# A transformer block on one core: the first transposed blocks copied in two pieces, two first projections done block by block, and a new list of tasks

## The chip, the cores and the metric

The kernel runs on one core of one Trainium2 chip. The metric is the device time of one execution in microseconds. Each of the core's engines (TensorE or PE, VectorE or DVE, ScalarE or ACT, GpSimd or POOL, and SyncE or SP, which here only issues DMAs) runs its own instructions in order, and they meet at semaphores.

## The reference, cut to what matters

```python
x = A_x                                     # 1 x 2048 x 640, bf16
h  = x + A(layernorm(x))
h2 = h + silu(layernorm(h) @ w1) @ w2       # 640 -> 1728 -> 640

def A(x):                                   # 32 heads of 20, 4 segments of 512 tokens
    q, k, v = x @ wq, x @ wk, x @ wv
    for s in range(4):                      # M (20x20 a head) and z carry over
        p = softmax(qs @ ks.T * scale + causal_mask)
        a_mem = (phi(qs) @ M) / (phi(qs) @ z + 1e-6)     # phi(t) = t+1 if t>0 else exp(t)
        o = g * a_mem + (1 - g) * (p @ vs)               # g = sigmoid(beta), a head
        M, z = M + phi(ks).T @ vs, z + sum(phi(ks))
    return o @ wo
```

## The kernel before, in words

**Staging.** The 2048 tokens are 16 blocks of 128, four to a segment; a block lies in the 128 partitions. The weights stay in on-chip memory, and every array goes to and from DRAM once. A block is normalized in `layer_norm` (statistics `st` and `r`, then `ap`, which writes bf16 rows `xn_rot`), and its transpose (feature on the partitions) is what the projections and the first FFN product read. The first four blocks are transposed on TensorE: `tp` multiplies by the identity, five matmuls of 128 columns into two PSUM banks, and `te` copies the five chunks into `hT` (lines 786 and 787: one instruction on ScalarE or on VectorE). All other blocks are transposed by a DMA, `tr` (line 792). `wq` and `wk` are rearranged after loading, one chunk of 128 rows at a time (`re_w`, lines 691 and 693), so that four heads stand at partitions 0, 32, 64 and 96 of a product.

**Attention.** For each segment s, `pr` (line 859) are ten projections of q and k (five chunks c, w = 0 for q and 1 for k), 512 columns each; in segment 0 each is two halves, x (blocks 0 and 1) and y (2 and 3). `qe` (lines 867, 868) copies a product from PSUM. `v` and `ve` do the same for the values. Twelve small DMAs a segment, `vt` (line 899), move the heads that did not fit in the five chunks to three further ones, and `vp` does so for phi(q). For eight groups of four heads: `qk` (line 949) writes scores into four PSUM banks, four heads at a time on four row tiles of TensorE; `e` (line 961) is the exponential on ScalarE, either one instruction over four banks (128x2048, with a + in its name) or two over two banks each (128x1024); `mk` masks the diagonal on GpSimd; `av` multiplies by the values, four column tiles at once; `oe` scales and copies that product, `tn` transposes it back, `nm` normalizes, `ad` adds the memory part. `pha`, `phb` and `ex` make phi; `kt` transposes phi(k) by a DMA (line 1192), `kg` and `kh` gather its left-over heads, and `mz`, `ma`, `mb` update M and z.

**Behind it.** `ot` (line 1249) transposes the attention rows of a block by a DMA, `wo` (line 1257) multiplies them by `wo` into two banks, `rs` adds x. After the second layer norm, `h1` (line 1292, 14 chunks; segment 0 in two halves) and `th`, `s` (silu), then `h2` (line 1334; four tasks a block, `h2_b_0` to `h2_b_3`; the last also reads `w_w2_5` if the block is odd), `o` (residual) and `out` (store). `w_w1_*` and `w_w2_*` are the loads of the FFN weights (line 580).

**What sets the order.** Every step is a task of a graph. The order of all tasks, the engine of those that have a choice, and the buffers are a list, `ORDER`, of words `name/engine:slots`: A is ScalarE, D VectorE, G GpSimd, S SP; slots are buffer or PSUM bank numbers, in the order in which the task first needs them. `wo11:6` is the product of block 11 in banks 6 and 7. Each engine takes its tasks in the list's order; `Tracker` puts in the semaphore waits that reads, writes and reused buffers need. A PSUM bank can thus be written again only when the engine that read it last is done. `fill29:0` is 29 matmuls on TensorE into bank 0 that nobody reads, at the start. DMAs are issued by SP or ScalarE, in their place in that engine's list.

The tasks that the prediction follows: `w_w2_5` and `h2_1_3`, `ot2` and `wo2`, the twelve `vt` of segment 1 and `qk13a0` (the first scores that read them), `n1_tr8` to `n1_tr11` and `pr220`, `av24`, `av25`, `oe24`, `oe25` and `wo11`, and at the front `n1_tp0`, `n1_tp1`, their copies `te` and the first projections.

Of the kernel before, what the change touches and what calls it, by code (L numbers as in the profile page):

```python
# [324 lines left out]
D = 640  # L325
# [6 lines left out]
NC = D // 128  # L332
# [10 lines left out]
SPLIT0 = tuple((c, w) for c in range(5) for w in range(2))  # L343
HALVES = True
# [117 lines left out]
def build(nc, es, A_x, A_wq, A_wk, A_wv, A_wo, A_beta, B_x, B_w1, B_w2, out):  # L462
# [340 lines left out]
    def declare_front(s):  # L803
# [5 lines left out]
        for i in range(4):  # L809
            layer_norm("n1_", 4 * s + i, X[4 * s + i], [0], xTa, xT_, i, k0 + P["ln1"] + P["ln1s"] * i if s else -30 + i)  # L810
# [599 lines left out]
```

## Time and profile before

| | |
|---|---|
| time, median of 3 runs (lowest, highest) | 300.31 us (299.82, 300.44) |
| the profiled execution's own time | 301.21 us |
| its span, and what lies around it | 299.5 us, 1.7 |
| granted TensorE clock | 1.00 |
| busy in the span: PE, DVE, ACT, POOL | 286.4, 219.3, 219.2, 137.9 us |
| exponentials on ACT (line 961) | 152.2 us |

The page's line "span" gives the stretch from the first to the last recorded instruction, and engines' busy time as a share of it. In a timeline a row is a run of like instructions: start and length in us, engine, line, what it computes, how many; in brackets stands how long the engine was idle just before it and what ended that. SPq is the queue of DMA issues on SP. The lines themselves stand in the prediction.

### The profile page before, as it was taken

Reading aid. Unit: us, or ns where it says so; the run is one execution under the profiler, and the core shown is the slowest. Engines: PE = TensorE matmul, PEld = TensorE weight load, DVE = VectorE, ACT = ScalarE, POOL = GpSimd, SP = SyncE. Lnnn points to the kernel's source line nnn. Section 1 sums busy time; section 2 is a strip of 40 time slices with the busy share of each in tenths; the row PEclk is TensorE's granted clock in tenths of the full one; section 3 lists DMA queues with packets and bytes.
Section 4 is the critical chain, followed back from the end, with each engine's and each line's share of the span. In section 5 each row is a group of like instructions: output and inputs, shape, how many; then the busy total and the mean of one; then the engine's idle time right before and its main releaser. Section 6 shows DMA issues by size and latency. Waiting matters only on the chain.

```text
span 299.5 us, 7397 instructions
## 1 busy us (share of the span) xinstructions
PE 286.4 (96%) x2980; PEld 167.7 (56%) x2980; DVE 219.3 (73%) x499; ACT 219.2 (73%) x266; POOL 137.9 (46%) x256
## 2 busy tenths in 40 slices
PE   8898799999998999999999999999999999999997
PEld 6685454545664554666653444456665457754575
DVE  4798768877777878899689875757977677835522
ACT  4985998999997989999889888978786840013500
POOL 4247873545643688636465445625675620200000
DMA  7945745264835241052552300173242012321002
GB/s 214 363 137 100 176 87 182 47 166 124 149 62 85 45 109 30 4 104 50 98 145 55 75 2 2 20 91 70 51 71 46 9 37 53 90 66 44 25 22 88
DMA packets 49905, 25.38 MB, mean 85 GB/s; under 512 B 39488, under 2 KB 48032, under 8 KB 49872
## 3 DMA queue, kind: packets, MB, share of 16 engines
q1 hardware_dynamic: 47944, 22.74, 33.9%
q10 hardware_dynamic: 1928, 2.18, 2.6%
q8 instruction: 23, 0.38, 0.6%
q14 instruction: 10, 0.08, 0.1%
HBM read 10.41 MB, written 2.62 MB: 44 GB/s over the span
## 4 chain that ended last, share of the span: by engine, by line
PE 67%; DVE 9%; SPq 7%; ACT 7%; DMA 5%; issue 2%; POOL 0%; ACTq 0%; DVEq 0%
PE ps_all L1334 18%; PE ps_all L1292 14%; PE ps_all L859 9%; PE ps_all L1257 7%; PE ps_all L949 6%; ACT PT L961 5%; PE ps_all L993 5%; PE ps_all L820 4%; SPq L899 4%; DMA x_tok<-in_A_x_dram 2%; DMA oT<-otok 2%; PE ps_all L1023 1%; SPq L792 1%; DVE stt L741 1%; SPq L580 1%
## 5 line engine op out<-in xcount | busy, mean ns | idle before, releaser
L961 ACT ACTIVATE PT<-ps_all 128x1024 bf16<-128x1024 f32 (+1 forms) x114 | 152.2, 1369 | 15.5 <-PE ps_all L949 14.8
L972 POOL TENSOR_SCALAR_AFFINE_SELECT PT<-PT 128x512 bf16<-128x512 bf16 x128 | 81.3, 646 | 66.6 <-ACT PT L961 64.6
L1334 PE MATMUL ps_all<-w_sb,sT 128*128 128x320 bf16 (+2 forms) x462 | 65.3, 295 | 0.6 <-DMA w_sb<-in_B_w_dram 0.4
L1292 PE MATMUL ps_all<-hT,w_sb 128*128 128x512 bf16 (+1 forms) x325 | 62.5, 337 | 0.5 <-DVE sT L1307 0.3
L1301 ACT ACTIVATE th<-ps_all 128x512 f32<-128x512 f32 (+2 forms) x70 | 33.3, 502 | 38.9 <-PE ps_all L1292 33.1
L1334 PEld LDWEIGHTS ps_all<-w_sb,sT 128*128 128x128 bf16 x462 | 43.1, 98 | 19.2 <-issue 1.3
L1307 DVE SCALAR_TENSOR_TENSOR sT<-th,ps_all 128x512 bf16<-128x512 f32 (+2 forms) x70 | 38.0, 561 | 17.1 <-ACT th L1301 16.0
L1292 PEld LDWEIGHTS ps_all<-hT,w_sb 128*128 128x128 bf16 x325 | 29.8, 98 | 26.1 <-issue 3.3
L762 POOL TENSOR_TENSOR rst<-rst,eps_c 128x1 f32<-128x1 f32 x32 | 18.6, 580 | 27.7 <-DVE rst L756 26.2
L741 DVE BATCH_NORM_STATS2 stt<-x_tok 128x6 f32<-128x320 bf16 x62 | 27.2, 480 | 1.7 <-DMA x_tok<-in_A_x_dram 1.3
L1257 PE MATMUL ps_all<-wo_sb,oT 128*128 128x320 bf16 x160 | 24.3, 299 | 1.2 <-DMA oT<-otok 0.6
L1055 POOL TENSOR_TENSOR otok<-on 128x320 bf16<-128x320 bf16 x24 | 19.1, 799 | 11.1 <-DVE on L1047 11.1
L1347 DVE SCALAR_TENSOR_TENSOR x_tok<-ps_all,x_tok 128x640 bf16<-128x640 f32 (+3 forms) x18 | 13.1, 744 | 13.8 <-PE ps_all L1334 13.8
L1047 DVE TENSOR_TENSOR on<-ps_all,rd 128x640 bf16<-128x640 f32 x24 | 19.8, 824 | 0.9
L1257 PEld LDWEIGHTS ps_all<-wo_sb,oT 128*128 128x128 bf16 x160 | 14.9, 98 | 8.7 <-issue 2.1
L820 PE MATMUL ps_all<-wv_sb,xT 128*128 128x320 bf16 x120 | 18.3, 299 | 0.9 <-ACT PT L961 0.5
L859 PE MATMUL ps_all<-xT,wkr 128*128 128x512 bf16 x75 | 18.6, 380 | 0.1
L868 DVE CAST QK<-ps_all 128x512 bf16<-128x512 f32 x22 | 15.0, 688 | 4.8 <-PE ps_all L859 4.6
L768 DVE TENSOR_SCALAR xn_rot<-x_tok,mvt,rst 128x640 bf16<-128x640 bf16 x32 | 15.5, 489 | 3.8 <-POOL rst L762 2.6
L859 PE MATMUL ps_all<-xT,wqr 128*128 128x512 bf16 x75 | 18.2, 380 | 0.0
L1265 DVE TENSOR_TENSOR x_tok<-ps_all,x_tok 128x640 bf16<-128x640 f32 x16 | 13.1, 817 | 7.0 <-PE ps_all L1257 6.9
L993 PE MATMUL ps_all<-PT,Vx 128*32 128x512 bf16 (+3 forms) x384 | 16.4, 301 | 0.0
(104 smaller groups left out, 336.6 us busy)
## 6 DMA issues: line engine op xcount, KB each, us to landing
w_sb<-in_B_w_dram SPq DMA_DIRECT2D x5, 432.0 KB, 4.4
w_sb<-in_B_w_dram SPq DMA_DIRECT2D x3, 480.0 KB, 4.0
x_tok<-in_A_x_dram SPq DMA_DIRECT2D x2, 640.0 KB, 6.9
out_dram<-x_tok SPq DMA_DIRECT2D x8, 160.0 KB, 1.9
out_dram<-x_tok ACTq DMA_DIRECT2D x7, 160.0 KB, 1.8
wo_sb<-in_A_wo_dram SPq DMA_DIRECT2D x1, 800.0 KB, 10.8
QKV<-QK SPq DMA_DIRECT2D x11, 72.0 KB
sT<-in_A_wq_dram SPq DMA_DIRECT2D x2, 320.0 KB, 3.9
```

The lines of the kernel that those rows point to most:

```text
L741: T.add(DV, lambda e, hh=hh: e.bn_stats(out=stt[:, s, 6 * hh:6 * hh + 6], in_=xb[:, 320 * hh:320 * hh + 320]), reads=R((xa, xsub)), writes ...
L820: fns.append(lambda e, c=c, hh=hh: e.matmul(bank(ps, hh)[:, 0:320], lhsT=xT_[:, c, 128 * i:128 * i + 128], rhs=wv_sb[:, c, 320 * hh:320 * ...
L859: fns = [lambda e, kc=kc: e.matmul(bank(ps)[:, lo:hi], lhsT=wt[:, kc, c, :], rhs=xT_[:, kc, lo:hi], start=(kc == 0), stop=(kc == NC - 1)) ...
L961: T.add(AC, lambda e: e.activation(out=pt[:, pta.slot, q0:q0 + nq, 0:width], in_=sc3[:, b0:b0 + nq, 0:width], func=ACT.Exp, scale=SCALE), ...
L972: T.add(PO, lambda e: e.affine_select(out=v, in_=v, pattern=[[0, 4], [1, 128]], compare_op=ALU.is_ge, fill=0.0, base=0, channel_multiplier ...
L993: fns.append(lambda e, j=j, r=r, h=h, pa=pa, pt=pt, co=co, q0=q0, ji=ji: e.matmul(bank(po)[32 * r:32 * r + 32, q0:hi], lhsT=Vx[:, vx.slot, ...
L1047: T.add(DV, lambda e: e.tensor_tensor(out=on[:, ona.slot, :, :].rearrange("p b (x e) -> p b x e", e=DH), in0=v[:, :, :, 0:DH], in1=r2.unsq ...
L1257: fns.append(lambda e, c=c, hh=hh: e.matmul(bank(ps, hh)[:, 0:320], lhsT=oT[:, c, 128 * i:128 * i + 128], rhs=wo_sb[:, c, 320 * hh:320 * h ...
L1292: fns = [lambda e, c=c: e.matmul(bank(ps)[:, lo:hi], lhsT=w1_sb[:, c, 128 * f:128 * f + 128], rhs=hT[:, c, lo:hi], start=(c == 0), stop=(c ...
L1301: T.add(AC, lambda e: e.activation(out=th[:, tha.slot, lo:hi], in_=bank(ps)[:, lo:hi], func=ACT.Tanh, scale=0.5), reads=R((ps, [0])), writ ...
L1307: T.add(DV, lambda e: e.scalar_tensor_tensor(out=sT[:, f, lo:hi], in0=th[:, tha.slot, lo:hi], scalar=1.0, in1=bank(ps)[:, lo:hi], op0=ALU. ...
L1334: fns.append(lambda e, f=f, t0=t0, fr=fr, hh=hh, n=n: e.matmul(bank(pa, hh)[:, 0:n], lhsT=sT[:, f, t0:t0 + 128], rhs=w2_sb[:, fr, c0 + 320 ...
```

## The change

Three things change.

First, the copies of the transposed blocks 0 and 1 are each two tasks: `te0a` takes chunks 0 to 2, `te0b` chunks 3 and 4. The list puts te0a, te0b and te1a on ScalarE and te1b on VectorE; before, te0 was on VectorE and te1 on ScalarE. What reads `hT` in segment 0 now waits for both pieces (`XS`).

Second, the two projections named in `FIRST`, pr010x and pr040x (the query halves of chunks 1 and 4), are done block by block: five matmuls of 128 columns for block 0 and five for block 1, where there were five of 256 columns. The first five wait for block 0 alone.

Third, the whole list is another one. It begins with `fill30:7`, 30 filler matmuls where there were 29, and ends with `fill2:2` for `fill2:6`. 40 of the 80 exponentials of score tiles are one instruction over four banks, where 46 were.

```diff
+FIRST = ("010x", "040x")
...
-            def e_te(eng):
...
-                T.add(eng, f, reads=R((ps, [0])), writes=R((dstA, [i])))
-            G.task(f"{tag}te{b}", {AC: act_c(640), DV: dve_c(640)}, e_te, [(ps, [0])], [(dstA, [i])], prio)
+            for k, (c0, c1) in enumerate(((0, 3), (3, 5)) if b < 2 else ((0, 5),)):
+                ww = [(i, 0), (i, 1)] if b >= 2 else [(i, k)]
+
+                def e_te(eng, c0=c0, c1=c1, ww=ww):
...
+                    T.add(eng, f, reads=R((ps, [0])), writes=R((dstA, ww)))
+                n = 128 * (c1 - c0)
+                G.task(f"{tag}te{b}" + ("ab"[k] if b < 2 else ""), {AC: act_c(n), DV: dve_c(n)}, e_te, [(ps, [0])],
+                       [(dstA, ww)], prio)
...
+        XS = lambda bs: list(bs) if s else [(i, h) for i in bs for h in (0, 1)]
...
+                        if tag in FIRST:
+                            for i in range(b0, b1):
+                                t0 = 128 * i
+                                T.run(PE, [lambda e, kc=kc, t0=t0: e.matmul(
+                                    bank(ps)[:, t0:t0 + 128], lhsT=wt[:, kc, c, :], rhs=xT_[:, kc, t0:t0 + 128],
+                                    start=(kc == 0), stop=(kc == NC - 1)) for kc in range(NC)],
+                                    R((xTa, XS([i])), (W[wk_], [c])), R((ps, [0])))
+                            return
-                        T.run(PE, fns, R((xTa, range(b0, b1)), (W[wk_], [c])), R((ps, [0])))
+                        T.run(PE, fns, R((xTa, XS(range(b0, b1))), (W[wk_], [c])), R((ps, [0])))
```

Of the list, two lines near the tasks av24, av25 and wo11:

```diff
-ot8 mk26b_0 av24:6 oe24/A:0 vt39/S kh23/D phb330 phb221 kt22:0 e26a2 qk26e0:0 e26e2:0 wo11:6 e26e0 mk26e_0 mk26e_256
+h2_4_2 mk25b_0 mk25b_384 qk26a0:2 e26a2:4 h2_4_3 o4 vt34/S kg22/G av25:7 e26a0 mk26a_0 av24:5 vt31/S oe25/A:1 oe24/D:0
```

In the old list av25:7 and oe25/D stand in the line before the first of these.

**SP's queue around ot3 and ot2.** The next two pieces are SP's rows from ot3 (before: the row ahead of the first one shown) to ot2, the last row in each. L899 and L914 are the `vt`, L792 and L798 the DMA transposes `n1_tr`, L1192 and L1207 is kt13, L1249 and L1264 is `ot`, L580 and L581 are loads of w2. Before:

```order
L792 DMA_TRANSPOSE xT<-xn_rot 128x5x128
L899 DMA QKV<-QK 12x3x1024
L899 DMA QKV<-QK 8x2x1024 x2
L792 DMA_TRANSPOSE xT<-xn_rot 128x5x128
L899 DMA QKV<-QK 8x1x1024 x3
L792 DMA_TRANSPOSE xT<-xn_rot 128x5x128
L1192 DMA_TRANSPOSE phiKt<-phiK 128x4x128
L899 DMA QKV<-QK 8x2x1024
L899 DMA QKV<-QK 12x3x1024
L580 DMA w_sb<-in_B_w_dram 64x640
L899 DMA QKV<-QK 8x1x1024
L1249 DMA_TRANSPOSE oT<-otok 128x5x128
```

Of the changed kernel, again from the row after ot3:

```order
L914 DMA QKV<-QK 12x3x1024
L581 DMA w_sb<-in_B_w_dram 128x3x640
L914 DMA QKV<-QK 8x1x1024
L798 DMA_TRANSPOSE xT<-xn_rot 128x5x128 x2
L914 DMA QKV<-QK 8x1x1024
L914 DMA QKV<-QK 8x2x1024
L798 DMA_TRANSPOSE xT<-xn_rot 128x5x128
L1207 DMA_TRANSPOSE phiKt<-phiK 128x4x128
L914 DMA QKV<-QK 8x2x1024 x2
L914 DMA QKV<-QK 12x3x1024
L914 DMA QKV<-QK 8x1x1024
L1264 DMA_TRANSPOSE oT<-otok 128x5x128
```

The load `L580 DMA w_sb<-in_B_w_dram 64x640`, which is w_w2_5, is no longer among them: it now stands twenty rows ahead of ot2 (row 31 of SP, ot2 being row 51 in both). One three-chunk load of w2 (w_w2_3) stands there now. Of the transposes n1_tr, three stand here in both lists; the fourth (n1_tr9 before, n1_tr10 now) follows behind ot2, before it ahead of kt12 and now behind it.

**ScalarE's first rows.** L786 and L790 are the `te`, L691 and L692 the rearrangement of wq and wk, L867 and L882 the copies `qe` of projections. Before:

```order
L733 ACTIVATE otok,mvt<-x_tok 128x640
L736 ACTIVATE otok,mvt<-x_tok,mvt 128x640
L786 ACTIVATE hT<-ps_all 128x5x128
L691 ACTIVATE wqr<-sT 128x5x4x20
L691 ACTIVATE wqr<-sT 128x5x4x12
L691 ACTIVATE wqr<-sT 128x5x4x20
L691 ACTIVATE wqr<-sT 128x5x4x8
L691 ACTIVATE wqr<-sT 128x5x4x4
L867 ACTIVATE w_sb<-ps_all 128x256
L691 ACTIVATE wkr<-sT 128x5x4x20
L691 ACTIVATE wkr<-sT 128x5x4x12
L867 ACTIVATE w_sb<-ps_all 128x256 x6
```

Of the changed kernel:

```order
L734 ACTIVATE otok,mvt<-x_tok 128x640
L737 ACTIVATE otok,mvt<-x_tok,mvt 128x640
L790 ACTIVATE hT<-ps_all 128x3x128
L790 ACTIVATE hT<-ps_all 128x2x128
L790 ACTIVATE hT<-ps_all 128x3x128
L692 ACTIVATE wqr<-sT 128x5x4x20
L692 ACTIVATE wqr<-sT 128x5x4x8
L692 ACTIVATE wqr<-sT 128x5x4x4
L882 ACTIVATE w_sb<-ps_all 128x256 x2
L692 ACTIVATE wkr<-sT 128x5x4x20
L692 ACTIVATE wkr<-sT 128x5x4x12
L882 ACTIVATE w_sb<-ps_all 128x256 x5
```

One copy of five chunks became three pieces, and two of the rearranged rows of wq went to VectorE.

**ScalarE's exponentials in segment 0.** L961 and L976 are the exponentials of scores, 128x2048 if over four banks and 128x1024 if over two; L834 is `ve`, L1222 and L1237 `ma00`, L874 and L889 `ex`. Before, from e0y1 on:

```order
L961 ACTIVATE PT<-ps_all 128x2048
L647 ACTIVATE zf<-beta_bc 128x32
L834 ACTIVATE Vx<-ps_all 128x32x20
L961 ACTIVATE PT<-ps_all 128x1024 x2
L961 ACTIVATE PT<-ps_all 128x2048
L961 ACTIVATE PT<-ps_all 128x1024 x2
L961 ACTIVATE PT<-ps_all 128x2048
L1222 ACTIVATE Mz<-ps_all 128x2x84
L961 ACTIVATE PT<-ps_all 128x1024 x2
```

Of the changed kernel, from e0y1 on:

```order
L976 ACTIVATE PT<-ps_all 128x1024 x2
L976 ACTIVATE PT<-ps_all 128x2048 x2
L889 ACTIVATE ex<-w_sb 128x512
L976 ACTIVATE PT<-ps_all 128x1024 x2
L976 ACTIVATE PT<-ps_all 128x2048
L1237 ACTIVATE Mz<-ps_all 128x2x84
L976 ACTIVATE PT<-ps_all 128x1024 x4
L976 ACTIVATE PT<-ps_all 128x2048
```

The exponential of e4x1, two halves before, is one instruction of four banks, and stands directly ahead of that of e4x2; e0y1 is two halves now.

218 lines of the change are left out of this document (109 added, 109 removed).

## The prediction

> **What bounds the kernel now.** I read the page's first line and the busy time of each engine by stage first, to see which engine is short of time where.
>
> ```profile
> span 299.5 us, 7397 instructions
> ...
> 30.00:74.00 44.00, 39.90 (x540) 22.10 (x530) 34.48 (x86) 41.12 (x43) 25.79 (x50) 1.00 0.51 131
> 74.00:86.00 12.00, 11.65 (x155) 7.36 (x153) 8.91 (x22) 11.97 (x17) 7.01 (x16) 1.00 0.65 119
> 86.00:97.00 11.00, 9.91 (x104) 5.40 (x101) 7.97 (x19) 9.13 (x12) 3.71 (x8) 1.00 0.48 79
> 97.00:155.00 58.00, 57.49 (x659) 33.30 (x659) 49.82 (x117) 51.96 (x61) 36.03 (x59) 1.00 0.32 62
> ...
> 240.00:283.00 43.00, 42.88 (x282) 25.14 (x281) 27.08 (x50) 10.48 (x19) 4.24 (x8) 1.00 0.22 51
> ```
>
> The columns are start and end, length, then busy time of TensorE, its weight loads, VectorE, ScalarE and GpSimd, the granted clock (1.00 everywhere), DMA share and GB/s. Three regimes show. From 30 to 86 us ScalarE is the fuller engine: 41.12 of 44 and then 11.97 of 12 us. From 97 us on TensorE is full: 57.49 of 58, and 42.88 of 43 near the end. Between them, at 86 to 97, neither is: TensorE stands still for 1.09 us and ScalarE for 1.87. A reordering can win nothing in the last regime, because TensorE's work is the same; it can win in the gap, and in the first 86 us if it lightens ScalarE.
>
> So next I looked at what TensorE waits for in the gap, in its timeline, and at what the SP queue did before that.
>
> ```profile
> 86.24 0.40 PE L949 MATMUL ps_all<-QK 20*128 20x512 bf16 x4
> 86.57 1.53 PE L1257 MATMUL ps_all<-wo_sb,oT 128*128 128x320 bf16 x10
> ...
> 90.90 1.26 PE L1334 MATMUL ps_all<-w_sb,sT 128*128 128x320 bf16 x8 [0.43 <-DMA w_sb<-in_B_w_dram]
> ...
> 93.13 1.53 PE L1257 MATMUL ps_all<-wo_sb,oT 128*128 128x320 bf16 x10 [0.65 <-DMA oT<-otok]
> ...
> 97.35 0.40 PE L949 MATMUL ps_all<-QKV 20*128 20x512 bf16 x4
> ```
>
> ```profile
> 72.56 0.58 SPq L580 DMA_DIRECT2D w_sb<-in_B_w_dram  x1
> ...
> 74.06 1.23 SPq L1249 DMA_TRANSPOSE oT<-otok  x1
> 75.40 1.22 SPq L792 DMA_TRANSPOSE xT<-xn_rot  x1
> 76.67 2.31 SPq L899 DMA_DIRECT2D QKV<-QK  x3
> 79.02 2.24 SPq L792 DMA_TRANSPOSE xT<-xn_rot  x1
> 81.31 2.00 SPq L899 DMA_DIRECT2D QKV<-QK  x3
> 83.35 1.20 SPq L792 DMA_TRANSPOSE xT<-xn_rot  x1
> 84.60 1.27 SPq L1192 DMA_TRANSPOSE phiKt<-phiK  x1
> 85.91 1.57 SPq L899 DMA_DIRECT2D QKV<-QK  x2
> 87.52 1.62 SPq L580 DMA_DIRECT2D w_sb<-in_B_w_dram  x1
> 89.19 0.68 SPq L899 DMA_DIRECT2D QKV<-QK  x1
> 89.91 1.21 SPq L1249 DMA_TRANSPOSE oT<-otok  x1
> 91.16 1.28 SPq L792 DMA_TRANSPOSE xT<-xn_rot  x1
> ```
>
> SP issues without a pause: the rows of its timeline join end to end from 74.06 to 91.16. Both things that TensorE waits for are in that queue's tail: w_w2_5 (87.52) feeds h2_1_3 at 90.90, and ot2 (89.91) feeds wo2 at 93.13. So here the length of SP's list is the bound. The two waits sum to 0.43 + 0.65 = 1.08 us.
>
> **The change part by part.** The sum is made against the profiled execution, 301.21 us (its span of 299.5 and 1.7 around it); it lies 0.9 above the median of 300.31, so I take the difference over to the median.
>
> *SP's list from ot3 to ot2.* Before, 14 issues stand from ot3 up to ot2, w_w2_5 among them. Now w_w2_5 is issued some twenty issues earlier, ahead of kt03, and from ot3 up to ot2 stand ot3, eight vt, w_w2_3, three transposes n1_tr and kt13. By the pitches of the rows: ot3 1.34 (74.06 to 75.40), a vt 0.75 ((2.35 + 2.04 + 1.61) / 8), an n1_tr 1.25, kt13 1.31, a w2 load 0.63 (72.56 to the next start, by its row 0.58 and the 0.05 that follows each). That is 1.34 + 6.00 + 3.75 + 0.63 + 1.31 = 13.03 us, so ot2 issues at 74.06 + 13.03 = 87.1, not 89.91: one vt fewer (0.75), and the two slow issues of before, 79.02 (2.24, about 1.0 over its kind) and 87.52 (1.62, 1.0 over), not counted. It landed 3.18 after its issue (next fence), so now at 90.3; wo2, with both waits gone, is wanted at 93.13 - 1.08 = 92.05. The wait goes, and so does that of h2_1_3. If two issues are slow again, ot2 lands at 92.3, and 0.25 stays. I take -1.08, with -0.83 and 0 as the poor ends.
>
> ```profile
> 25.15 3.39 DMA w_sb<-w_sb
> ...
> 89.91 3.18 DMA oT<-otok
> ```
>
> What is late next: qk13a0 at 97.35 needs all twelve vt. The last now follows ot2, kt12, n1_tr10 and vt15: 87.1 + 1.25 + 1.31 + 1.25 + 0.75 = 91.7, landing 3.39 later (a like transfer, the first row) at 95.0, wanted at 96.3. Then n1_tr10 itself, wanted by pr220: issued at 89.7 against 91.16 for the last n1_tr of before. Past 97 TensorE is full, so a shift at 93 reaches the end.
>
> *ScalarE's load before 86 us.* Off it go ve01, ve10, qe120 and ma01, on it comes qe101.
>
> ```profile
> L834 ACT ACTIVATE Vx<-ps_all 128x640 bf16<-128x640 f32 x3 | 2.2, 722 | 0.0
> L867 ACT ACTIVATE QK<-ps_all 128x512 bf16<-128x512 f32 x8 | 4.8, 601 | 0.5 <-PE ps_all L859 0.4
> L1222 ACT ACTIVATE Mz<-ps_all 128x168 f32<-128x168 f32 x2 | 0.6, 308 | 0.1
> ```
>
> 2 x 0.72 + 0.60 + 0.31 - 0.60 = 1.75 us less. VectorE takes it in 34.48 of 44 us. How much arrives is between nothing (another engine holds the stage) and 1.75. Only the stretch of 74 to 86 has no ScalarE idle time at all, and of the moved ones ma01 stands next to it; I take -0.3.
>
> *wo11 near 201.* Before, wo11 writes banks 6 and 7, and the later of the two copies that free them (oe24) is on ScalarE.
>
> ```profile
> 201.29 2.88 PE L1257 MATMUL ps_all<-wo_sb,oT 128*128 128x320 bf16 x20 [0.51 <-ACT oTs L1006]
> ```
>
> Now av24 lies in bank 5, so that wo11 waits for oe25 alone, which comes first. 0 to -0.5; oe25 sits behind an exponential on ScalarE, so -0.2.
>
> *More changes between tile shapes on TensorE.* Counting qk (four row tiles), av and h1_*_13 (four column tiles) and the rest (whole array) in both lists, the shape changes 195 times where it did 192. The four qk matmuls at 86.24 let the next task begin 0.33 later (86.57), though 512 columns at that next row's rate (ten of 320 columns in 1.53 us, 0.48 ns a column) take 0.24: about 0.1 for a change. Three more: +0.3, or 0 where TensorE waits anyway.
>
> *The front.* Block 0's copy, one CAST on VectorE, becomes two on ScalarE; block 1's, one on ScalarE, becomes one on each.
>
> ```profile
> 5.42 0.19 POOL L752 TENSOR_SCALAR rst<-mvt 128x1 f32<-128x1 f32 x1 [0.42 <-ACT otok L736]
> ...
> 6.42 0.37 PEld L777 LDWEIGHTS ps_all<-ident,xn_rot 128*128 128x128 bf16 x5
> ...
> 7.00 0.82 DVE L787 CAST hT<-ps_all 128x640 bf16<-128x640 f32 x1
> ...
> 7.45 0.70 ACT L786 ACTIVATE hT<-ps_all 128x640 bf16<-128x640 f32 x1 [2.12 <-PE ps_all L777]
> ...
> 8.30 2.34 PE L859 MATMUL ps_all<-hT,wqr 128*128 128x256 bf16 x20 [0.89 <-ACT hT L786]
> ...
> 10.15 0.74 DVE L693 COPY wkr<-sT 128x400 bf16<-128x400 bf16 x4 [1.27 <-DMA sT<-in_A_wk_dram]
> ...
> 10.62 1.81 PE L859 MATMUL ps_all<-hT,wkr 128*128 128x256 bf16 x15
> ...
> 10.97 0.89 DVE L741 BATCH_NORM_STATS2 stt<-x_tok 128x6 f32<-128x320 bf16 x2
> ```
>
> ScalarE's three copies are bounded by 0.70 each, and by 0.70 for two together; take 1.2 in all: from about 7.1 to 8.3, against 8.15 before. Block 0 is whole by about 7.9, so pr010x can start on it at about 8.2, when its weights' copies (VectorE, after te1b) are there: a gain of 0.1 at most. One filler more, 30 for 29 (the list has no six fewer), puts the transposes at 6.6; behind that hides that ap0 now stands behind r1 on VectorE, which waits for ScalarE's statistics until 5.42. But whatever is won here meets the key weights, which VectorE gets at 10.15 from the DMA, and blocks 2 and 3, whose statistics start at 10.97: the three projections of k start at 10.62 in either case. I take 0; up to 0.4 late passes there too.
>
> *Queue moves that I cost at nothing.* x8 and w_w1_0 go ahead of the vt on SP, and w_w2_0 ahead of n2_tr1 and n2_tr0, so that a load is issued before the transposes on which the first h1 tasks wait. By the two rows of such loads (72.56 and 87.52) each holds SP for 0.6 to 1.6 us; these are the bounds on the h1 side, beside 0. I take 0, because the h1 tasks fall into the stage of 30 to 74 us, in which ScalarE and not TensorE is the fuller engine and 3.9 of 44 us of TensorE are idle already.
>
> Sum: -1.08 - 0.3 - 0.2 + 0.3 + 0 = -1.28, 301.21 to 299.93, and the median to 299.0.
>
> **The rivals.**
>
> *SP's order does not matter.* The DMA engines are busy for 0.65 of 74 to 86 us; were landing, not issuing, the limit, ot2 would come when it did, and only -0.3 - 0.2 + 0.3 is left: 300.1. Against it: ot2 took 3.18 us to land, of 19 us in the queue. The Trainium skill, "DMA: Bandwidth & Descriptors", section "Issuing engines are not separate DMA queues", says that time on the issuing sequencer is usually small beside the transfer; by that rule this rival is the forecast. The trace differs: 15.85 us of issues stand against 3.18 of landing. Chance 0.10.
>
> *The wait forms anew at qk13a0.* If two issues are slow again, the last vt lands at 97.0, 0.75 late, and 0.25 of ot2's wait stays: -0.28, 300.0. Chance 0.14.
>
> *Slower: the exponentials take turns with TensorE.* A score task whose banks the exponential just before it on ScalarE still reads cannot start until that one ends; ScalarE then idles.
>
> ```profile
> 33.29 3.71 ACT L961 ACTIVATE PT<-ps_all 128x1024 bf16<-128x1024 f32 x3 [0.51 <-PE ps_all L949]
> ...
> 47.48 1.88 ACT L961 ACTIVATE PT<-ps_all 128x2048 bf16<-128x2048 f32 x1 [0.50 <-PE ps_all L949]
> ```
>
> These are two such pairs, e4x3 after e4x2 and e4ya after e3ya. In the new list ten pairs have nothing between them on ScalarE, six before (the first new one: e4x2 after e4x1, one instruction of four banks where it was two halves). Four more at 0.5 are +2.0; with -1.08 + 0.3 that is +1.2, 301.5 for the median. It decides from the third new pair that TensorE has no other work for. Against it: before 86 us the count is two in both. Chance 0.17.
>
> *ScalarE's relief arrives whole:* -1.08 - 1.75 = -2.8, 297.5. Chance 0.08.
>
> **How the numbers follow.** The forecast has 0.51, with its own range of 298.3 to 299.8 (relief 0 to -0.8, shape changes 0 to 0.3). The range of 297.8 to 301.2 holds it, both no-change rivals and the near part of the slow and of the fast one. A measurement of this kernel can tell about 0.2%, 0.6 us. Faster: 0.51 + 0.08, less 0.01 of the forecast's upper end, 0.58. Slower: 0.17 and 0.01 of unnamed ends, 0.18. The same: 0.24.
>
> **What would show it.** Right: ot2 issued 2 us or more sooner after ot3 than 15.85, no DMA named ahead of h2_1_3 and wo2, the k projections still starting near 10.6, wo11's wait under 0.3. Wrong: TensorE waits of half a microsecond on ScalarE's exponentials at new places, a wait of qk13a0 on QKV, hT late at the first h1, or the first k projection past 11.0.

## The result and the profile after

The changed kernel takes 298.33 us (median of 5, 297.27 to 298.85) against 300.31 (299.82 to 300.59) for the kernel before: a ratio of 0.9932, 95% interval 0.9914 to 0.9949. Beside the last three experiments both were timed again: 297.69 (6 runs) against 300.26 (17 runs), 0.9917 (0.9898 to 0.9936). The prediction was 299.0. In the profiled executions the difference is larger, a span of 296.6 against 299.5. In some executions the granted clock falls for a few microseconds and the time is mostly 1 to 2.5 us longer: so in the profiled ones of a_nosplit and a_tr7 (0.87 and 0.86 from 24 to 33 us) and of a_actback (0.58 from 46 to 50 us), of which only stretches outside the fall are compared, and in four of the six of a_actback, whose two at a clock of 1.00 took 301.66 and 302.52.

The stages of the changed kernel, in the columns of the table by stage that the prediction shows:

```profile
span 296.6 us, 7437 instructions
...
30.00:74.00 44.00, 40.44 (x550) 22.80 (x543) 36.63 (x91) 41.45 (x48) 25.50 (x46) 1.00 0.54 117
74.00:86.00 12.00, 11.90 (x160) 7.43 (x158) 11.07 (x26) 11.62 (x17) 7.43 (x13) 1.00 0.76 139
86.00:97.00 11.00, 10.51 (x115) 6.13 (x113) 10.30 (x23) 10.18 (x9) 6.21 (x15) 1.00 0.41 78
97.00:155.00 58.00, 57.61 (x652) 32.86 (x650) 48.44 (x110) 51.40 (x64) 33.72 (x57) 1.00 0.35 74
...
240.00:283.00 43.00, 43.00 (x285) 26.13 (x284) 25.73 (x48) 11.45 (x20) 3.51 (x7) 1.00 0.23 54
```

As the clock is the same and TensorE's work nearly so, the stages that gained are those in which TensorE is busy for longer: 40.44 for 39.90 from 30 to 74 us, 11.90 for 11.65, and 10.51 for 9.91 in the gap. From 97 to 155 and from 240 to 283 us, where TensorE was already full, little was won (57.61 for 57.49, 43.00 for 42.88).

A sharper reading is the start of one and the same task in two traces. The difference of the starts is how far TensorE is ahead; where it changes, time was won or lost. The last three columns are two traces that were taken later: b_unmerge, an experiment whose list is that of before but for six exponentials, and a second profile of the changed kernel.

| task | before | after | lead | b_unmerge | after again | lead |
|---|---|---|---|---|---|---|
| pr011x, first projection of k | 10.62 | 10.50 | -0.12 | 10.66 | 10.64 | -0.02 |
| qk4ya0 | 47.03 | 47.06 | +0.03 | 47.39 | 46.70 | -0.69 |
| qk11a0 | 86.24 | 85.01 | -1.23 | 86.43 | 84.66 | -1.77 |
| wo2 | 93.13 | 90.59 | -2.54 | 92.15 | 90.24 | -1.91 |
| qk13a0 | 97.35 | 94.96 | -2.39 | 96.67 | 94.60 | -2.07 |
| av19 | 151.11 | 148.67 | -2.44 | 150.20 | 148.23 | -1.97 |
| qk25a0 | 183.06 | 181.16 | -1.90 | 182.14 | 180.45 | -1.69 |
| wo11 | 201.29 | 199.02 | -2.27 | 200.37 | 198.30 | -2.07 |
| qk31a0 | 235.20 | 232.77 | -2.43 | 234.28 | 232.06 | -2.22 |
| last h2 | 296.77 | 293.89 | -2.88 | 295.51 | 293.18 | -2.33 |

In both pairs 1.1 to 1.3 us are won between qk4ya0 and qk11a0. In the gap, from qk11a0 to qk13a0, the first pair shows 1.16 and the second 0.30; that is the row on which the prediction's main term stood, and the pairs do not agree on it (further traces of this stage stand under b_w2early). Some 0.3 to 0.5 is lost between av19 and qk25a0, and about 0.4 comes back up to wo11. Behind wo11 the lead grows by another 0.61 and 0.26; no wait of TensorE over 0.15 us stands there in any of the four traces, and where it comes from was not looked into.

The gap in TensorE's timeline of the changed kernel, and SP's queue there (ot3 at 72.98, ot2 at 86.93):

```profile
88.27 2.07 PE L1349 MATMUL ps_all<-w_sb,sT 128*128 128x320 bf16 x14
90.27 0.39 PE L964 MATMUL ps_all<-QK 20*128 20x512 bf16 x4
90.59 1.53 PE L1272 MATMUL ps_all<-wo_sb,oT 128*128 128x320 bf16 x10
...
93.49 0.46 PE L1225 MATMUL ps_all<-Vx,phiKt 128*128 128x84 bf16 x8 [0.37 <-DVE x_tok L1280]
...
94.96 0.39 PE L964 MATMUL ps_all<-QKV 20*128 20x512 bf16 x4
```

```profile
72.98 1.28 SPq L1264 DMA_TRANSPOSE oT<-otok  x1
...
76.56 3.27 SPq L798 DMA_TRANSPOSE xT<-xn_rot  x2
...
83.90 2.99 SPq L914 DMA_DIRECT2D QKV<-QK  x4
86.93 1.21 SPq L1264 DMA_TRANSPOSE oT<-otok  x1
```

Both waits of before are gone, at h2_1_3 and at wo2, and none formed at qk13a0; a new one of 0.37 stands at 93.49, where mz10 writes a bank that VectorE frees late. SP needs 13.95 us from ot3 to ot2, where it needed 15.85; in the second profile it needs 13.33. (The prediction had 13.03; two transposes took 3.27, where it counts 2.50.)

### The profile page after: what moved, and what is told of

Its sections match the earlier page's. It is cut to its first block, busy times and chain, and to the rows that moved or that the text cites. A ratio compares the mean times of both kernels' runs of the same rounds, so it can differ in the third digit from the quotient of the medians.

```text
span 296.6 us, 7437 instructions
## 1 busy us (share of the span) xinstructions
PE 285.0 (96%) x2991; PEld 167.6 (56%) x2991; DVE 222.8 (75%) x506; ACT 217.5 (73%) x266; POOL 139.9 (47%) x257
## 4 chain that ended last, share of the span: by engine, by line
PE 76%; DVE 8%; DMA 7%; ACT 4%; POOL 2%; issue 2%; SPq 1%; DVEq 0%; ACTq 0%
PE ps_all L1349 19%; PE ps_all L1307 15%; PE ps_all L866 12%; PE ps_all L1272 7%; PE ps_all L964 7%; PE ps_all L827 5%; PE ps_all L1008 5%; ACT PT L976 3%; DMA x_tok<-in_A_x_dram 3%; DMA xT<-xn_rot 2%; PE ps_all L1038 1%; DMA w_sb<-w_sb 1%; PE ps_all L1092 1%; PE ps_all L1225 1%; POOL PT L987 1%
## 5 line engine op out<-in xcount | busy, mean ns | idle before, releaser
L976 ACT ACTIVATE PT<-ps_all 128x1024 bf16<-128x1024 f32 (+1 forms) x120 | 153.1, 1310 | 17.7 <-PE ps_all L964 16.5
L1316 ACT ACTIVATE th<-ps_all 128x512 f32<-128x512 f32 (+2 forms) x70 | 34.0, 505 | 35.1 <-PE ps_all L1307 31.0
L1362 DVE SCALAR_TENSOR_TENSOR x_tok<-ps_all,x_tok 128x640 bf16<-128x640 f32 (+3 forms) x18 | 13.3, 745 | 16.7 <-PE ps_all L1349 16.6
L883 DVE CAST QK<-ps_all 128x512 bf16<-128x512 f32 x23 | 15.7, 688 | 8.8 <-PE ps_all L866 8.7
L842 DVE CAST Vx<-ps_all 128x640 bf16<-128x640 f32 x15 | 12.3, 819 | 5.9 <-PE ps_all L827 5.8
L769 DVE TENSOR_SCALAR xn_rot<-x_tok,mvt,rst 128x640 bf16<-128x640 bf16 x32 | 14.8, 473 | 1.7 <-POOL rst L763 1.0
```

Of the source, the lines that this page charges most:

```text
L976: T.add(AC, lambda e: e.activation(out=pt[:, pta.slot, q0:q0 + nq, 0:width], in_=sc3[:, b0:b0 + nq, 0:width], func=ACT.Exp, scale=SCALE), ...
L1316: T.add(AC, lambda e: e.activation(out=th[:, tha.slot, lo:hi], in_=bank(ps)[:, lo:hi], func=ACT.Tanh, scale=0.5), reads=R((ps, [0])), writ ...
```

## The experiments

Twelve runs were made, in three batches; the letter b means the kernel before with an edit, a the changed kernel with one, and after_again is the changed kernel as it is. Ratios are to the kernel before, timed beside them.

| run | median us | ratio, 95% interval |
|---|---|---|
| b_w2early | 300.45 | 0.9999 (0.9980 to 1.0018) |
| b_act | 303.64 | 1.0095 (1.0067 to 1.0123) |
| b_unmerge | 300.84 | 1.0010 (0.9986 to 1.0035) |
| b_split | 301.61 | 1.0020 (0.9999 to 1.0041) |
| b_cover | 300.96 | 1.0021 (1.0003 to 1.0038) |
| a_nosplit | 298.78 | 0.9954 (0.9937 to 0.9971) |
| a_merge | 299.45 | 0.9966 (0.9936 to 0.9996) |
| a_actback | 303.29 | 1.0077 (1.0049 to 1.0105) |
| a_tr7 | 298.28 | 0.9934 (0.9908 to 0.9959) |
| a_w2late | 298.09 | 0.9930 (0.9906 to 0.9953) |
| a_best | 298.11 | 0.9933 (0.9915 to 0.9952) |
| after_again | 297.69 | 0.9917 (0.9898 to 0.9936) |

The theory to be tested was the prediction's: SP's list is what ends the waits of the gap, and ScalarE's load is what the stage before it lacks. The rivals were that landing and not issuing counts, that the profiled execution of before was out of the ordinary, and that halves or order, not load, made the stage of ScalarE shorter.

### b_w2early: the load alone

```diff
-mk10e_256 n2_st3:6 w_w2_5 h2_1_3
+mk10e_256 n2_st3:6 h2_1_3
-epsg1 w_w2_1/S
+epsg1 w_w2_5 w_w2_1/S
```

> The kernel before, with one DMA moved: w_w2_5 stands on SP's list just ahead of w_w2_1, at a place where SP idles, and no longer two issues ahead of ot2. If the length of SP's list is what ends the two waits of the gap (my theory), h2_1_3 no longer waits for a DMA, ot2 is issued 0.7 to 1.6 us sooner (by whether the moved load's issue was slow) and wo2's wait of 0.65 is nearly gone: the time falls by 0.4 to 1.1 us, to 299.2 to 299.9. Rival, that landing and not issuing is the limit: only the wait of h2_1_3 (0.43) goes and comes back as a longer one of wo2, and the time stays at 300.3. Second rival, that the profiled execution of before was out of the ordinary in its gap: no wait of this size stands there in most executions, and the time stays too.

The time stayed: 0.9999. In its trace both waits of the gap are gone, and wo2 starts 0.97 earlier than in the profile of before. But b_unmerge, sent in the same batch and with SP's list as before, shows the same: wo2 at 92.15. First b_unmerge's SP queue, then TensorE in b_w2early at the end of the gap (wo2 at 92.16):

```profile
87.26 0.54 SPq L580 DMA_DIRECT2D w_sb<-in_B_w_dram  x1
87.84 0.69 SPq L899 DMA_DIRECT2D QKV<-QK  x1
88.58 1.21 SPq L1249 DMA_TRANSPOSE oT<-otok  x1
...
92.46 0.71 SPq L899 DMA_DIRECT2D QKV<-QK  x1
```

```profile
91.84 0.40 PE L949 MATMUL ps_all<-QK 20*128 20x512 bf16 x4
92.16 1.53 PE L1257 MATMUL ps_all<-wo_sb,oT 128*128 128x320 bf16 x10
...
96.69 0.40 PE L949 MATMUL ps_all<-QKV 20*128 20x512 bf16 x4 [0.43 <-DVE rst L756]
```

The issue of w_w2_5 took 0.54 in b_unmerge where it took 1.62 in the profile of before. With the short issue ot2 comes in time there and the two waits do not exist; 0.43 of wait then stands at qk13a0. (The trace names VectorE's rst as its releaser, but qk13a0 reads only what the vt bring; the last of them is issued at 92.46 in b_unmerge, and I read the wait as the landing of that one.)

That does not make the waits those of one execution. Three more experiments have the old order from ot3 to ot2, and in each TensorE waits for ot2 again. First b_split, then b_cover's TensorE and b_cover's SP queue:

```profile
92.99 1.53 PE L1272 MATMUL ps_all<-wo_sb,oT 128*128 128x320 bf16 x10 [0.72 <-DMA oT<-otok]
```

```profile
93.00 1.53 PE L1257 MATMUL ps_all<-wo_sb,oT 128*128 128x320 bf16 x10 [0.51 <-DMA oT<-otok]
```

```profile
87.99 0.55 SPq L580 DMA_DIRECT2D w_sb<-in_B_w_dram  x1
...
89.31 1.22 SPq L1249 DMA_TRANSPOSE oT<-otok  x1
```

| trace (us) | issue of w_w2_5 | ot3 to ot2 on SP | landing of ot2 | wait at wo2 | wait at qk13a0 | qk11a0 to qk13a0 |
|---|---|---|---|---|---|---|
| before | 1.62 | 15.85 | 3.18 | 0.65, and 0.43 at h2_1_3 | 0.13 | 11.11 |
| b_split | 1.43 | 15.59 | 3.21 | 0.72, and 0.12 at h2_1_3 | 0.13 | 10.88 |
| b_cover | 0.55 | 14.64 | 3.64 | 0.51 | 0.13 | 10.37 |
| b_act | 0.55 | 14.49 | 3.58 | 0.19 | 0.18 | 10.19 |
| b_unmerge | 0.54 | 14.32 | 2.61 | none | 0.43 | 10.24 |
| b_w2early | moved | 14.01 | 2.81 | none | 0.43 | 10.24 |
| the changed kernel, its second profile and six edits of it | moved, in a_w2late 0.54 | 13.32 to 14.39 | 2.70 to 3.46 | none | none | 9.94 or 9.95 |

So with the old order wo2 waits for ot2 in four of five traces, by 0.19 to 0.72, and in the fifth qk13a0 waits instead, as the prediction's rival of qk13a0 had it. A slow issue of w_w2_5 is one way to the wait; a slow landing is another (b_cover: issue 0.55, landing 3.64), so the rival of landing holds in part. With the new list ot2 lands 0.42 to 1.50 us ahead of wo2 in all eight traces. The new order ends the waits, and is worth 0.25 to 1.17 in this stage, 0.43 in the middle one of the five. The second rival holds for the size alone: the profile of before had, in sum, the largest waits of the five. Why ot2 lands faster in most traces of the new list was not found.

The load alone (b_w2early) takes away the waits at h2_1_3 and wo2 and leaves 0.43 at qk13a0. Its stage is 0.87 shorter than that of before, but only 0.13 shorter than the middle one of the five, and the interval of its time, 0.2% or 0.6 us to either side, can't tell that from nothing.

### a_w2late: the load back in the new list

```diff
-kt01:0 w_w2_5 h1_0_4_0:7
+kt01:0 h1_0_4_0:7
-h2_1_2 vt11/S h2_1_3
+h2_1_2 w_w2_5 vt11/S h2_1_3
```

> The changed kernel with w_w2_5 put back near ot2 on SP's list, ahead of vt11. Theory (SP's list ends the wait): ot2 is issued 0.6 us later where the load's issue takes 0.54 and 1.6 later where it is slow; it landed 1.0 us ahead of its need (89.63 against 90.59), so no wait in the first case and 0.6 in the second, and 0.2 to 0.6 us of wait at h2_1_3 if the load lands 3.1 to 3.3 us after an issue at 85.4 to 86: 0 to 0.9 slower than the changed kernel. Rival: no change at all (0.2), as w_w2_5 moved forward did nothing for the kernel before.

The ratio was 0.9930 where the unedited changed kernel had 0.9917, well inside both intervals. Its issue took 0.54, ot2 went out at 87.31 and wo2 started without a wait at 90.47; the wait of 0.37 at mz10 stayed. ot2 landed 0.42 ahead of wo2, the least of the eight traces with the new list. The place of this one load is worth nothing that can be measured, in either list.

### b_unmerge and a_merge: halves of exponentials

In the kernel before, six exponentials as halves:

```diff
-e2ya+:5
+e2ya2:5 e2ya0
-e4y1+:6
+e4y10:6 e4y12
...
```

> The kernel before, with six exponentials of segment 0 and 1 (e2ya, e3ya, e4ya, e4y1, e4y3, e8a) done as two halves in the order of the changed kernel instead of one instruction over four banks. If halves are what closes the waits of TensorE for the exponentials and ScalarE's idle time there (1.3 us of waits of TensorE, 1.9 of ScalarE between 47 and 87 us), TensorE is 0.4 to 0.9 us ahead at 80 us. Rival, smaller load of ScalarE: nothing, or later by the six extra instructions, about 0.06 us each by 2 x 0.97 against 1.88 for one: 0.4 us slower.

Nothing: 1.0010, and TensorE stands where it stood until 86 us (qk11a0 at 86.43 for 86.24; from qk4ya0 to qk11a0 it needs 39.04, and 39.10 to 39.21 in before, b_w2early and b_split). In the changed kernel the same six were joined:

```diff
-e4y10:5 e4y12
+e4y1+:5
-e8a0:2 e8a2
+e8a+:2
...
```

> The changed kernel with six of its exponentials between 38 and 67 us (e2ya, e3ya, e4ya, e4y1, e4y3, e8a) joined again into one instruction over four banks, as before; each stands where its second half stood. If the halves close the waits of TensorE and ScalarE between 47 and 80 us, 0.5 to 1.2 us of the lead of 1.23 are gone at 80 us. Rival: it is the order (other work of ScalarE between two exponentials of the same banks, and between the first and second half), not the halves as such, since halves alone did nothing in the kernel before: within 0.3 us at 80 us, or a little faster, by 6 x 0.06.

The time rose to 0.9966, though the interval touches the changed kernel's. From qk4ya0 to qk8a0 it needs 19.05 us (46.74 to 65.79), and 18.29 in the second profile of the changed kernel (46.70 to 64.99). The same 0.76 stands between its 38.71 from qk4ya0 to qk11a0 and the 37.95 or 37.96 of four traces with halves (after, after_again, a_w2late, a_best). It falls at one place of TensorE's timeline, ahead of qk6ya0:

```profile
55.95 0.40 PE L964 MATMUL ps_all<-w_sb 20*128 20x256 bf16 x8 [0.90 <-ACT PT L976]
```

There e4y1 as one instruction holds banks 4 to 7 until its end, and qk6ya0 writes 2 to 5. So halves are worth 0.76 us in the new list and at most 0.17 in the old one: they pay where the next score task in the list wants just the banks that the first half frees.

### b_act and a_actback: the engines of five tasks

```diff
-ve01/A ... ve10/A ... qe101/D:0 ... qe120/A ... ma01/A:2,3
+ve01/D ... ve10/D ... qe101/A:0 ... qe120/D ... ma01/D:2,3
```

> The kernel before, with only the engines of five tasks changed as in the changed kernel: ve01, ve10, qe120 and ma01 from ScalarE to VectorE, qe101 from VectorE to ScalarE; order and buffers as before. If the lead that TensorE gains between 47 and 80 us comes from ScalarE's smaller load, 0.3 to 1.2 us of it show here and at 86 us TensorE is that much ahead. Rival, that the lead comes from exponentials done in halves, which free two of the four banks sooner: nothing or under 0.3 us here.

It became slower by 1.0%. TensorE in b_act, at 49 to 57 us:

```profile
51.26 0.40 PE L949 MATMUL ps_all<-w_sb 20*128 20x256 bf16 x12 [1.57 <-ACT PT L961]
...
57.07 0.40 PE L949 MATMUL ps_all<-w_sb 20*128 20x256 bf16 x12 [1.47 <-DVE QK L868]
```

The old list has qe101 ahead of e4ya. On VectorE it delayed nobody; on ScalarE it waits there for its projection, with the exponential behind it, and qk0y30 waits 1.57 us for that exponential's banks. The second is qe120, now on VectorE behind qe121, which waits for its own projection. The reverse edit, in the changed kernel:

> The changed kernel with five tasks on the engine that they had before: ve01, ve10, qe120 and ma01 on ScalarE, qe101 on VectorE. Theory (the prediction's relief of ScalarE): 1.75 us more of work for ScalarE, which has no idle time from 47 to 87 us in the changed kernel but 0.18; what falls there (qe120, ma01, less qe101: 0.3) shows in full, 0.3 later at 86 us, and what falls before 47 us (ve01, ve10: 1.4) in part: 0.3 to 1.7 slower in all. Rival: the places in the list matter and not the engines; within 0.2 us.

It is slower too: 1.0077 of the kernel before, where the changed kernel has 0.9932 and 0.9917; a part of that is the granted clock. Two waits of the same kind stand in the trace, wo1 behind ve10 and, at 58.66, a score task behind qe120:

```profile
46.26 4.55 PE L1272 MATMUL ps_all<-wo_sb,oT 128*128 128x320 bf16 x20 [1.82 <-ACT Vx L841]
...
58.66 0.40 PE L964 MATMUL ps_all<-w_sb 20*128 20x256 bf16 x12 [1.35 <-ACT QK L882]
```

The 4.55 us of the first row, 2.88 elsewhere, go with the granted clock of 0.58 from 46 to 50 us and not with the edit. Neither theory had this: one expected 0.3 to 1.7 us, the other under 0.2, and with the clock at 1.00 it is over 3. An engine in such a list is chosen together with the place: the wrong one costs 1.4 to 1.8 us at one spot, and the sum of durations that the prediction made (1.75 us of relief) says nothing of it.

### b_cover: other work between two exponentials

```diff
-th0_5_0:0 qk4y30:2 ... e4y3+:5 ... th0_6_0:1
+th0_5_0:0 qk4y30:2 ... th0_6_0:1 e4y3+:5
-e4y1+:6 ex120:0 ... e8a+:3
+e4y1+:6 ... ex120:0 e8a+:3
```

> The kernel before with two tasks moved on ScalarE: th0_6_0 ahead of the exponential of e4y3 and ex120 ahead of that of e8a, where it then has other work while TensorE writes the scores into the banks that the exponential before has just left (in the kernel before ScalarE idles 0.20 and 0.43 us ahead of these two). Theory: the lead of the changed kernel between 57 and 80 us comes from such cover; about 0.4 to 0.6 us of it show at 67 us. Rival: TensorE's waits there are for ScalarE's whole work, which is the same, and other idle time takes their place: within 0.15 us at 67 us.

The theory fell: slower, 1.0021, and 0.43 us are lost at qk8a0 by a new wait:

```profile
66.65 0.40 PE L949 MATMUL ps_all<-QK 20*128 20x512 bf16 x4 [0.43 <-DVE sT L1307]
```

ScalarE's timeline of b_cover shows why:

```profile
64.35 0.38 ACT L1301 ACTIVATE th<-ps_all 128x256 f32<-128x256 f32 x1 [0.43 <-DVE sT L1307]
64.63 1.87 ACT L961 ACTIVATE PT<-ps_all 128x2048 bf16<-128x2048 f32 x1
```

At its new place th0_6 waits 0.43 itself, for the step of VectorE that frees its buffer, and holds up the exponential of e4y3 behind it, which ends at 66.50; qk8a0 writes two of that one's banks and starts at 66.65. (The row names VectorE's sT; the banks come free with the exponential.)

### b_split and a_nosplit: the first two parts alone and left out

```diff
-n1_te1/A:0 n1_te0/D
+n1_te0a/A:0 n1_te0b/A n1_te1b/D n1_te1a/A
```

with the changed code of the two functions.

> The kernel before with its own list and only the first two parts of the change: the copies of the first two transposed blocks in two pieces each, on the engines that the changed kernel has, and the two projections done block by block. I expect what the prediction took for the front, 0: the first three projections of k still start near 10.6 us, and 300.3 stays within 0.3. Rival: the lead of 0.46 us that the changed kernel has at 16 to 20 us comes from these two parts, and TensorE is ahead by 0.3 to 0.5 us at 20 us.

The old list with these two parts starts its first projection of k at 11.10 and not at 10.62. This is not the parts' doing, though. The 29 fillers took 6.10 us in this execution and 5.57 in the profile of before, and b_act, whose front is the old one, starts as late behind fillers of 6.23. First b_split, then b_act:

```profile
1.12 6.10 PE L619 MATMUL ps_all<-zpad 128*128 128x256 bf16 x29 [1.12 <-DVE zpad L596]
...
11.10 1.80 PE L866 MATMUL ps_all<-hT,wkr 128*128 128x256 bf16 x15
```

```profile
1.12 6.23 PE L618 MATMUL ps_all<-zpad 128*128 128x256 bf16 x29 [1.12 <-DVE zpad L595]
...
11.07 1.80 PE L859 MATMUL ps_all<-hT,wkr 128*128 128x256 bf16 x15
```

So the parts cost 0.1 us or nothing there (b_cover, old front, fillers of 6.15, starts at 10.99), and the trace has caught up by qk11a0 (86.32 for 86.24). The time, 1.0020, touches no change. For a_nosplit the edit is the reverse one, with te0 on ScalarE and te1 on VectorE.

> The changed kernel without its first two parts: te0 whole on ScalarE, te1 whole on VectorE, all first projections over both blocks; the new list otherwise. The front's term was 0. Theory: the two parts are worth up to 0.5 us at 20 us, and it is lost again by 47 us, where TensorE waits for the transpose of block 7 and for ScalarE, so the time stays at 298.3 within 0.3. Rival: the parts cost time here as they did with the old list (0.5 later at 10.6 us there), and the new list is 0.3 to 0.6 faster without them.

It gave 0.9954, beside a_tr7's 0.9934 in the same batch and the changed kernel's 0.9932 and 0.9917 in others; its interval overlaps with the first two and just misses the last. By the medians the two parts would be worth 0.2 to 0.4% in the new list, but the traces do not show it at the front: behind fillers of 6.15 and 6.11 us a_nosplit and a_tr7 start the first projection of k at 11.35 and 11.28, and, with the same fall of the clock between, wo11 at 201.19 and 201.13. (The "0.5 later" of the expectation's rival was the fillers'.)

### a_tr7, a_best and after_again: what could still be won

```diff
-e0y2+:6 w_w1_3 w_w1_1 mk0y2_0 kg00/G:0 mk0y2_256 n1_tr7
+e0y2+:6 n1_tr7 w_w1_3 w_w1_1 mk0y2_0 kg00/G:0 mk0y2_256
```

> The changed kernel with one DMA moved: n1_tr7, the transpose of block 7, on SP ahead of the two loads w_w1_3 and w_w1_1 and not behind them. In the changed kernel it is issued at 35.03, lands 7.37 us later, and v13 waits 1.31 for it at 42.45, and ScalarE then 1.30 at 44.36. Theory: the 432 KB loads ahead of it make its landing slow; ahead of them it lands within 3 to 5 us, before 40.9, the wait goes, and 0.6 to 1.3 us of it reach the end: 297.0 to 297.8. Rival: the landing stays slow, or TensorE waits at the next place (wo1 on ot1, the exponentials): under 0.3.

298.28 us, 0.9934: no gain over the changed kernel. The second profile of the changed kernel explains it, and a_merge, a_w2late and a_actback, with n1_tr7 at its old place, have no such wait at v13 either.

> The changed kernel once more, beside the others of this batch, for a second profile of it and its time on the same chip: 0.993 of before, within 0.002. In the trace, what is the same in both profiles is the kernel's, and what differs is of one execution: I expect the waits at v13 (1.31 in the first profile) and of VectorE for the load x12 (1.39) to differ, those on engines to be the same.

TensorE in the changed kernel's first profile, and after it in the second:

```profile
42.45 1.53 PE L827 MATMUL ps_all<-wv_sb,xT 128*128 128x320 bf16 x10 [1.31 <-DMA xT<-xn_rot]
```

```profile
43.55 0.40 PE L964 MATMUL ps_all<-w_sb 20*128 20x256 bf16 x8 [0.31 <-ACT PT L976]
54.06 0.95 PE L1092 MATMUL ps_all<-PT,Vx 128*32 128x256 bf16 x32 [0.16 <-DVE QK L883]
71.90 0.40 PE L964 MATMUL ps_all<-QK 20*128 20x512 bf16 x4 [0.24 <-DVE rd L1135]
93.13 0.46 PE L1225 MATMUL ps_all<-Vx,phiKt 128*128 128x84 bf16 x8 [0.37 <-DVE x_tok L1280]
```

The wait of 1.31 for the transpose of block 7 is not in the second one, while 0.16, 0.24 and 0.37 recur to the hundredth. The other wait that I took for one execution's does recur: VectorE stands still for the load x12 in both.

```profile
156.47 0.89 DVE L742 BATCH_NORM_STATS2 stt<-x_tok 128x6 f32<-128x320 bf16 x2 [1.39 <-DMA x_tok<-in_A_x_dram]
```

```profile
155.81 0.89 DVE L742 BATCH_NORM_STATS2 stt<-x_tok 128x6 f32<-128x320 bf16 x2 [1.19 <-DMA x_tok<-in_A_x_dram]
```

For a_best the statistics of block 12 were moved behind a silu step as well:

```diff
-x12/S n1_st12:6 n1_r12/G h1_1_1_0:4 th1_1_0:1 s1_1_0
+x12/S h1_1_1_0:4 th1_1_0:1 s1_1_0 n1_st12:6 n1_r12/G
```

> The changed kernel with two edits: n1_tr7 ahead of the loads w_w1_3 and w_w1_1 on SP, and the statistics of block 12 (n1_st12, with its r12) behind s1_1_0 on VectorE, which in the changed kernel waits 1.39 us for the load x12 in front of it. Theory: TensorE's wait of 0.38 at h1_1_8 goes, as does part of the 1.31 at v13: 0.3 to 0.9 faster than the changed kernel, 297.4 to 298.0. Rival: the wait for x12 comes back as a late transpose of block 12 (v30), or in the next step of VectorE, and that of v13 as one for ScalarE: within 0.2.

The wait for x12 went, but VectorE then waits for ScalarE in its place, and TensorE three times for VectorE:

```profile
155.69 0.69 DVE L1322 SCALAR_TENSOR_TENSOR sT<-th,ps_all 128x512 bf16<-128x512 f32 x1 [1.57 <-ACT th L1316]
```

```profile
159.74 1.25 PE L1307 MATMUL ps_all<-hT,w_sb 128*128 128x512 bf16 x5 [0.19 <-DVE sT L1322]
161.83 1.25 PE L1307 MATMUL ps_all<-hT,w_sb 128*128 128x512 bf16 x5 [0.51 <-DVE sT L1322]
163.31 1.52 PE L827 MATMUL ps_all<-wv_sb,xT 128*128 128x320 bf16 x10 [0.24 <-DVE sT L1322]
```

In this trace n1_tr7's part is worth 0.48 (qk4ya0 at 46.22 for 46.70, av19 at 147.71 for 148.23), but the changed kernel's own two profiles are 0.36 apart at qk4ya0, and by qk25a0 it is 0.42 behind (180.87 for 180.45). No edit of the changed kernel beat it.

## Why the prediction was right, and where it was not

The direction was right, and 298.33 lies in the forecast's own range of 298.3 to 299.8, at its very end. The size was not: -1.28 was forecast, and the two comparisons of medians give about -2.0 and -2.6; the second median, 297.69, lies below that range. (The range's two named terms give 298.2 to 299.3; its upper end needs the poor end of -0.83 and no gain at wo11 as well.) Term by term it was less good: errors of both signs cancelled in part, which is luck.

**SP's list, -1.08: the right waits, sized by one execution.** No DMA is named ahead of h2_1_3 or wo2 in any trace with the new list, and ot2 was issued 13.95 and 13.33 after ot3 (1.90 and 2.52 sooner than the 15.85, for a sign of 2 or more). In the pair of profiles the whole term came true (1.16 in the gap). As a term of the median it is smaller: over five traces with the old order the gap costs 0.25 to 1.17 more than with the new one, 0.43 in the middle, and moving w_w2_5 alone, in either list, showed nothing in the time. The prediction read the slow issue of 1.62 as part of the list's length. It had the two facts that speak against taking the wait over whole: the profiled execution lay 0.9 above the median, and the issue was, in its own words, 1.0 over its kind.

**ScalarE's load, -0.3: the step that failed.** The stage from qk4ya0 to qk11a0 gained 1.26 and 1.08, the largest steady gain of all, and the sum of durations that the term was made of is not what gained it. These are the waits of TensorE that the timeline of before names there:

```profile
59.41 1.41 PE L1292 MATMUL ps_all<-hT,w_sb 128*128 128x256 bf16 x10 [0.33 <-DVE sT L1307]
61.06 0.40 PE L949 MATMUL ps_all<-w_sb 20*128 20x256 bf16 x8 [0.24 <-ACT PT L961]
63.45 0.40 PE L949 MATMUL ps_all<-w_sb 20*128 20x256 bf16 x12 [0.25 <-ACT PT L961]
70.41 0.40 PE L949 MATMUL ps_all<-QK 20*128 20x384 bf16 x8 [0.20 <-DVE rst L756]
77.72 0.39 PE L949 MATMUL ps_all<-QK 20*128 20x512 bf16 x4 [0.24 <-ACT PT L961]
```

They sum to 1.26, and the two of the changed kernel (0.16 and 0.24) to 0.40, so they make 0.86 of the gain. What removed them is the list as a whole. Three single causes were tried in the old list, engines (b_act), halves (b_unmerge) and cover (b_cover); they gave 0.17 of the gain at most, and two cost time. In the new list the halves carry 0.76 of it, and the engines of the five tasks can't be put back there without new waits (a_actback). The rest was not taken apart, and stays open.

**wo11, -0.2:** between qk25a0 and wo11 the lead grows by 0.37 and 0.38, and the new timeline has no wait at wo11 (the row at 199.02). This is the same in every trace: 18.23 us and a wait of 0.51 in the six with the old list, 17.85 or 17.86 and no wait in the eight with the new one. The sign is as argued, the size between the 0.2 and the 0.51 of the old wait. No run tried it alone, so the bank and the engine are not told apart.

```profile
199.02 2.88 PE L1272 MATMUL ps_all<-wo_sb,oT 128*128 128x320 bf16 x20
```

**Changes of tile shape, +0.3:** not seen, and not tested by these lists. Two of the three added changes lie ahead of qk4ya0, where TensorE waits anyway, and one behind qk25a0; between qk4ya0 and qk25a0 both lists have 116.

**The front, 0:** right. The projections of k start at 10.50 and 10.64 (10.62 before), although the transposes start 0.5 earlier (6.02 for 6.52). That start is of the execution and not of the change: the 30 fillers took 4.87 to 6.15 us in eight traces, and where they took 6.11 (a_tr7) the transposes start at 7.08 and the projections of k at 11.28.

**Not forecast:** a loss of 0.54 and 0.28 between av19 and qk25a0, which begins with x12's wait on VectorE (0.25 in the profile of before, 0.46 in b_unmerge); a gain up to qk4ya0 that one slow transpose hid in the first profile of the changed kernel (0.1 to 0.7: 46.70, 46.74 and 46.94 in after_again, a_merge and a_w2late, 47.03 to 47.39 in the six traces with the old list); and the 0.61 and 0.26 behind wo11.

**The rivals.** That SP's order does not matter was given 0.10. The time of b_w2early and a_w2late is what it would give, but the traces speak against it: wo2 or qk13a0 waits in all five with the old order, neither in the eight with the new list. Its reason, the landing, is part of the cause all the same (2.61 to 3.64 with the old order). The Trainium skill, "DMA: Bandwidth & Descriptors", section "Issuing engines are not separate DMA queues", by which this rival went, calls the time on the issuing sequencer usually small beside the transfer. These traces differ where many issues stand in a row: 13.3 to 15.9 us of issues from ot3 to ot2, against the landing of 2.6 to 3.6. The wait at qk13a0 formed in b_unmerge and b_w2early, 0.43 each, where wo2 did not wait; the new list has none. Exponentials taking turns with TensorE cost one wait at qk3ya0 (0.31 at 43.55 in the second profile, 0.46 and 0.48 in a_w2late and a_best), in place of one of 0.52 that the kernel before has at qk4ya0, not four of 0.5 more.

## What to carry to other kernels

Take more profiles before a wait of one execution is put into a sum, and before it is struck out: three waits on engines recurred here to the hundredth, while the wait for ot2 was 0 to 0.72 in five traces of the same order, so neither the first trace nor the one without it gave its worth. Where the profiled execution lies above the median, look for the surplus in the very waits that you mean to remove. Compare a front only between executions that start alike: here the first projection of k lay between 10.50 and 11.28 with one and the same front, for the most part by the fillers. In a searched order, engine, place and buffers of a task belong together: five engines changed alone cost 1% in the old list, and time in the new one too.

## What the runs showed of the hardware

- The issue of one and the same DMA, w_w2_5, at the same place of SP's list, took 1.62 and 1.43 us in two traces (before, b_split) and 0.54, 0.55 and 0.55 in three (b_unmerge, b_act, b_cover). The landing of ot2 took 2.61 to 3.64 in the same five.
- The same filler matmuls at the start ran at different speeds at a granted clock of 1.00, and it differs by execution and not by kernel: 30 in 4.87 (after_again) to 6.15 us (a_nosplit), 29 in 5.57 (before) to 6.23 us (b_act).
- Within one execution the granted clock can fall for some microseconds and be 1.00 nearly everywhere else; a_tr7, 24 to 33 us (0.93 from 33 to 40):

```profile
24.00:33.00 9.00, 7.26 (x92) 4.16 (x94) 7.02 (x15) 4.80 (x5) 5.69 (x13) 0.86 0.64 107
```
